# A woven attention and maxout kernel: new order of the steps from batch 4's last sums on, and tiles in listed buffers

## The chip, the cores and the metric

The kernel runs on one core of one Trainium2 chip. The metric is the device time of one execution in microseconds, lower is better. The core has five engines with a queue of instructions each: TensorE (PE; its weight loads are shown apart as PEld), VectorE (DVE), ScalarE (ACT), GpSimd (POOL) and SyncE (SP), which here only issues DMAs. An engine works through its own queue in order; between engines, semaphores say what has to be finished first.

## What is computed

Attention with pooled keys and values over 8 batches, 8 heads, 576 tokens and 64 dimensions, then a maxout layer over all 8 x 576 = 4608 tokens with 512 channels and 768 hidden units. Cut to what matters:

```python
k_p = k.reshape(B, H, S // 8, 8, D).mean(axis=3)      # 72 keys per head
v_p = v.reshape(B, H, S // 8, 8, D).mean(axis=3)
scores = np.matmul(q, k_p.transpose(0, 1, 3, 2)) / np.sqrt(D)
attn = np.exp(scores - scores.max(-1, keepdims=True))
attn = attn / (attn.sum(-1, keepdims=True) + 1e-09)
x = np.matmul(attn, v_p)           # then (batch, token) x (head, dim)
h = np.maximum(np.maximum(x @ w1, x @ w2), x @ w3)
out = h @ w_out
```

## The kernel before

The work has two halves that run through each other. The attention goes by batches 0 to 7 of 576 tokens, the maxout layer by blocks 0 to 8 of 512 tokens, so a block needs tokens of one or two batches: block 5 needs batch 4 from its third chunk on and two chunks of batch 5, block 6 the rest of batch 5 and the first chunk of batch 6. Nothing is scheduled automatically. The order on every engine is the order in which the program emits its instructions, and that order is written out by hand as lists of short names. `MIDDLE` covers blocks 1 to 5 and the batches beside them, `ORDER` (run by `weave`) the outputs of block 5, the hidden part of blocks 6 to 8, the rest of batches 6 and 7 and the outputs of block 7. The emission order binds only instructions of one engine among themselves; a DMA on SP's queue, for instance, waits for the DMAs emitted before it on SP, and for its data.

A name with `-` emits the first part of a step, as a rule its matmuls, and parks its second part, as a rule the eviction of the PSUM result by ACT or DVE; the same name with `+` emits the parked part. Without a sign both follow at once. A number before a colon or stroke is the batch or the block:

- `b:T`, in `do`: one DMA transpose on SP of the whole query tile, `qT<-qb` (line 352). It needs batch b's q loaded. Batches 0 to 2 turn their queries on TensorE.
- `b:k`: three transposes of the pooled keys on TensorE and four copies into `kz` (line 215), all on ACT for batches 4 to 6, for batch 7 two on DVE and then two on ACT.
- `b:s0`, `b:s3`, `b:s6`: scores of three, three and two heads (line 229); their later parts are exponentials on ACT (line 234). Batch 7 instead has nine flat steps `s70` to `s78` of 512 columns, after batch 6's scores.
- `b:v0` to `b:v4`: attention times values for a chunk of 128 tokens (line 305), then reciprocal and product on DVE (lines 313, 315) give `xn`. `b:x0` to `b:x4`: a DMA transpose on SP of that chunk into the token buffer, `xT<-xn` (line 290), for batches above 2. In `ORDER` the colon is left out (`v62`, `x62`).
- `n/h`: one of a block's twelve hidden pieces, four matmuls of 512 columns (line 423); alternately ACT takes the relu of one (line 429) and DVE the maximum with the next (line 431). They use three PSUM buffers, tag `pw`.
- `n/1` to `n/7`: the seven products by which a block's output is formed, ten matmuls each (line 769), copied on ACT (line 780) or added on DVE (line 783). They need the sums `a1` to `a4` of tokens and `b1` to `b4` of hidden units (DVE, line 668). When all parts of a half are there, SP stores it (line 718). In `ORDER` these are `o1` to `o7`.
- In `ORDER`, `1a` to `7c`: seven products of four matmuls (line 846) for each of three groups a, b, c, that make blocks 6, 7 and 8's hidden units; ACT and DVE combine them (lines 823, 826, 855, 859). `T` forms the token differences they need (line 620), on DVE for block 6 and on GpSimd for blocks 7 and 8. `F` is half of an output tile of block 6 (lines 471, 475).
- `q7<`, `k7<`, `v7<`: GpSimd issues a load of that batch from memory, `q` of 576 KB with a cast to bf16, k and v with a cast to f16. It waits for the latest hidden piece or product emitted, and for the landing of the latest `T`. There are two buffers for each of q, k and v.
- `k6+2`, `v5+2`: the next two of the four additions by which GpSimd pools keys or values (lines 163, 163, 165, 167). `!` notes the latest DVE sum of those steps that take a gate; the next of these additions then waits for that sum. `f` is one difference of weights on DVE (lines 592, 601).

The tiles come from pools whose tags have a number of buffers that are used in rotation: PSUM has `att` (two), `pw` (three) and `tr` (one) while `MIDDLE` runs, and `pa`, `sc` (two each), `bc`, `po` and `val` (one each) while `ORDER` runs. A tile waits until the buffer's last tile has been read.

The names that the prediction uses: `5:x3`, `6:x0` and `7:T` on SP's queue, `s70` (`psf`), `2a`, `T`, the folds of `v 7` (`vpool`), block 4's products `4/3` and `4/4` with their stores.

Of the kernel before, what the change touches and what calls it, by code (L numbers as in the profile page):

```python
# [14 lines left out]
def kernel(
# [553 lines left out]
    pools.append(stage.enter_context(tc.tile_pool(name="psp", bufs=1, space=PSUM,  # L569
                                                  reuse_waits="tile")))  # L570
# [3 lines left out]

    def block(n, plan, stages):

        for slot, end in enumerate(part for stage in stages for part in stage(n)):
            if end:
                end()
            for b, steps in plan.get(slot, ()):  # L580
                if b < B:
                    do(b, steps)
# [476 lines left out]
```

## Time and profile before

| | us |
|---|---|
| runs of the kernel before | 226.75, 226.52, 225.45 (median 226.52) |
| profiled execution: span from the first to the last instruction | 224.5 |
| TensorE busy in the span | 213.0 |
| last matmul's end to the span's end (220.7 to 224.5) | 3.8 |
| a load of q, k, v from issue to landing (median of 7) | 7.7, 8.0, 11.9 |

The profiled execution is shown by its span; the runs' times also hold what lies before and after it, 2.0 us for the median. The profile's page has busy time by engine, groups of instructions by line, and DMA queues; the trace behind it also answers who waited for whom, and what ran in a stretch of time. Times in it are counted from the span's start. An instruction on SP is the issue of a DMA: its duration is how long the issue held SP, and the landing comes later. Matmuls overlap in the pipeline, so a row of four matmuls is longer than the distance to the next row. In brackets behind a row stands the idle time of its engine before it, and what ended that, as inferred from semaphores.

How the engines were busy over the span, in tenths, for 40 equal slices:

```profile
PE   7788999999999999999999999999799999999993
DVE  3658989037998795885679468629767977878940
ACT  2267524846784577266735845493694445564330
POOL 7974300999957969787685669794292903881020
DMA  6999999989749799739987998599420645200265
```

Counted from 0, slice 27 (from 151.5 us) begins the stretch in which the change's two lists meet; slices 28 and 29 are 157 to 168 us.

### The profile page before, as it was taken

What the parts mean: (1) busy time and instruction counts of PE and PEld (TensorE: products, weight loads), DVE (VectorE), ACT (ScalarE), POOL (GpSimd) and SP (SyncE); (2) the same over time, 40 slices, a digit from 0 to 9 for tenths busy, and PEclk for the clock granted to TensorE, in tenths of its full rate; (3) what the DMA queues carried; (4) which work ended last, traced back from release to release, by engine and by line L of the source; (5) the groups of instructions that cost most, each with busy time, mean ns of one, the idle gap of its engine ahead of it and who ended that gap; (6) DMA issues with size and microseconds to landing.
All of it is one profiled execution on the core that took longest, in us unless ns stands there. A gap on an engine that the chain in (4) does not pass through costs nothing.

```text
span 224.5 us, 4870 instructions
## 1 busy us (share of the span) xinstructions
PE 213.0 (95%) x1884; PEld 147.3 (66%) x1885; DVE 157.9 (70%) x308; ACT 123.2 (55%) x239; POOL 140.9 (63%) x121
## 2 busy tenths in 40 slices
PE   7788999999999999999999999999799999999993
PEld 2477744458659744964685478447589667788882
DVE  3658989037998795885679468629767977878940
ACT  2267524846784577266735845493694445564330
POOL 7974300999957969787685669794292903881020
PEclk9999999999999999999999999999999999999999
DMA  6999999989749799739987998599420645200265
GB/s 167 212 197 196 207 208 207 204 170 226 135 106 190 131 177 248 124 58 212 252 93 157 227 217 140 75 257 157 103 56 19 167 100 110 47 0 3 65 198 161
DMA packets 47303, 33.55 MB, mean 149 GB/s; under 512 B 26992, under 2 KB 42288, under 8 KB 47280
## 3 DMA queue, kind: packets, MB, share of 16 engines
q0 software_dynamic: 16944, 16.98, 47.2%
q1 hardware_dynamic: 29888, 15.87, 31.2%
q10 hardware_dynamic: 448, 0.39, 0.7%
q8 instruction: 15, 0.25, 0.4%
q14 instruction: 8, 0.07, 0.1%
HBM read 34.60 MB, written 9.44 MB: 196 GB/s over the span
## 4 chain that ended last, share of the span: by engine, by line
PE 69%; DMA 12%; POOL 8%; DVE 6%; ACT 2%; issue 1%; POOLq 0%; DVEq 0%; ACTq 0%
PE pw L423 22%; PE oA L769 13%; DMA vt<-in_v_dram 8%; PE oC L769 7%; PE pA L846 6%; DMA mw<-in_moe_w_dram 4%; PE pav L305 4%; PE oB L769 3%; PE psc L229 3%; PE po L475 3%; PE pC L846 3%; POOL half L163 2%; PE po L471 2%; DVE xn L315 1%; POOL mw L108 1%
## 5 line engine op out<-in xcount | busy, mean ns | idle before, releaser
L423 PE MATMUL pw<-xT,mw 128*128 128x512 f16 (+1 forms) x336 | 68.4, 349 | 0.2 <-ACT xT L299 0.2
L423 PEld LDWEIGHTS <-mw 128*128 128x128 f16 x336 | 30.7, 98 | 26.3 <-issue 1.8
L163 POOL TENSOR_TENSOR half<-vt 72x1024 f32<-72x1024 f16 (+1 forms) x12 | 29.1, 2443 | 20.5 <-DMA vt<-in_v_dram 13.2
L431 DVE TENSOR_TENSOR hT<-t,pw 128x512 f16<-128x512 f16 (+1 forms) x42 | 25.4, 608 | 21.4 <-PE pw L423 12.1
L234 ACT ACTIVATE et<-psc 72x512 f16<-72x512 f32 (+2 forms) x66 | 33.9, 571 | 9.0 <-PE psc L229 8.9
L165 POOL TENSOR_TENSOR half<-half 72x1024 f32<-72x1024 f32 (+1 forms) x13 | 28.1, 2165 | 10.4 <-DVE rcp L313 5.2
L429 ACT ACTIVATE t<-pw 128x512 f16<-128x512 f32 (+1 forms) x42 | 22.6, 538 | 17.0 <-PE pw L423 16.5
L315 DVE TENSOR_TENSOR xn<-pav,rcp 128x512 f16<-128x512 f32 x40 | 27.7, 691 | 1.4
L163 POOL TENSOR_TENSOR half<-ktFalse 96x768 f32<-96x768 f16 (+1 forms) x11 | 19.3, 1767 | 3.9 <-issue 3.8
L855 ACT CAST pad<-pA 128x512 f16<-128x512 f32 x27 | 15.1, 586 | 11.6 <-PE pA L846 9.1
L780 ACT COPY osb<-oA 128x512 f32<-128x512 f32 x20 | 11.8, 588 | 17.4 <-PE oA L769 17.2
L769 PEld LDWEIGHTS <-tt 128*128 128x128 f16 x200 | 18.9, 98 | 2.4
L229 PEld LDWEIGHTS <-kz 64*128 64x128 bf16 (+1 forms) x161 | 8.8, 95 | 12.4 <-issue 8.0
L305 PE MATMUL pav<-vp,et 72*128 72x65 f16 x320 | 16.4, 194 | 0.6 <-DVE xn L315 0.2
L305 PEld LDWEIGHTS <-et 72*128 72x128 f16 x320 | 15.0, 98 | 3.0 <-issue 1.3
L313 DVE RECIPROCAL rcp<-pav 128x8 f32<-128x8 f32 x40 | 8.1, 202 | 10.9 <-PE pav L305 10.8
L846 PEld LDWEIGHTS <-sw 128*128 128x128 f16 x144 | 13.8, 97 | 2.7 <-issue 0.2
L826 DVE SCALAR_TENSOR_TENSOR hT<-pad 128x512 f16<-128x512 f16 x18 | 14.0, 784 | 1.1 <-ACT pad L859 0.5
L823 DVE TENSOR_TENSOR pad<-pad,pC 128x512 f16<-128x512 f16 x18 | 12.3, 682 | 3.5 <-PE pC L846 2.7
L229 PE MATMUL psc<-qT,kz 64*128 64x256 bf16 (+5 forms) x138 | 13.2, 263 | 1.0 <-DVE qT L197 0.9
L620 POOL TENSOR_TENSOR pad<-xT 128x256 f16<-128x256 f16 x8 | 5.5, 689 | 13.0 <-DMA xT<-xn 13.0
L769 PEld LDWEIGHTS <-hT 128*128 128x128 f16 x126 | 12.3, 98 | 1.4
(122 smaller groups left out, 400.6 us busy)
## 6 DMA issues: line engine op xcount, KB each, us to landing
out_dram<-osb SPq DMA_DIRECT2D x32, 128.0 KB, 4.3
ktFalse<-in_k_dram POOLq DMA_DIRECT2D x7, 576.0 KB, 8.0
qb<-in_q_dram POOLq DMA_DIRECT2D x7, 576.0 KB, 7.7
vt<-in_v_dram POOLq DMA_DIRECT2D x7, 576.0 KB, 11.9
out_dram<-osb SPq DMA_DIRECT2D x11, 256.0 KB, 6.7
mw<-in_moe_w_dram POOLq DMA_DIRECT2D x9, 256.0 KB, 9.4
ktTrue<-in_k_dram SPq DMA_DIRECT2D x3, 384.0 KB, 5.4
out_dram<-ob SPq DMA_DIRECT2D x8, 128.0 KB, 2.8
```

What stands on the lines that cost most here:

```text
L163: yield e.tensor_tensor(out=f[:, at], in0=t[:, at, 0:4, :], in1=t[:, at, 4:8, :], op=ALU.add)
L165: yield e.tensor_tensor(out=f[:, :, 0:2, :], in0=f[:, :, 0:2, :], in1=f[:, :, 2:4, :], op=ALU.add)
L229: nc.tensor.matmul(out, kz_all[b % 2][f % 2][rows, h, :], qTs[b][rows, n + i0:n + i1, 64 * (h % 2):64 * (h % 2) + 64], start=True, stop=True)
L234: nc.scalar.activation(out=out, in_=in_, func=FT.Exp, scale=1.0 / 64.0)
L305: nc.tensor.matmul(pav[:, h // 4, 65 * (h % 4):65 * (h % 4) + 65], ets[b][:, h, c0:c0 + 128], vp_all[:, b, h, :], start=True, stop=True)
L315: nc.vector.tensor_tensor(out=xn, in0=pv[:, :, :, 0:D], in1=rcp.to_broadcast([128, 2, 4, D]), op=ALU.mult)
L423: mm = nc.tensor.matmul(pw, w_sb[wi][:, kc, bass.ts(jc, 128)], x[:, kc], start=(kc == 0), stop=(kc == KCH - 1))
L429: yield lambda t=t, pw=pw: nc.scalar.activation(out=t, in_=pw, func=FT.Relu)
L431: yield lambda t=t, pw=pw: nc.vector.tensor_tensor(out=hT[:, jc, c0:c1], in0=t, in1=pw, op=ALU.max)
L769: nc.tensor.matmul(p, left, right, stop=(r == 4), skip_group_check=True, start=(i in FIRST and r == 0 and (m == 0 or n == LAST)))
L846: mm = nc.tensor.matmul(p[:, w], a[:, kc, bass.ts(g, 128)], b[:, kc, :], start=(i in FIRST and w + kc == 0), stop=(w + kc == 2), skip_grou ...
L855: nc.scalar.copy(out=kept(i, g), in_=p)
```

## The change

Every step stays, with its instructions; the order and the buffers are new.

1. The hand-written plan of block 0 (`block`, with batch 1's first steps) becomes names at the head of `MIDDLE`, in the same order, with the loads of batch 3 and the folds of batch 2's k and v behind it (`k3<<` is a load without the waits). The folds of batches 1 and 2 keep their three additions, those above 2 their four.
2. From `5:T` on, `MIDDLE` is in a new order, and all of `ORDER` is. `4/3` and `4/4` are copied out and stored ahead of `5:x3` on SP, where they came behind `5:x4`; `q7<` and `v7<` stand between the additions of batch 6's values, where they came in block 5; `k7<` stands ahead of batch 5's last value additions; `7:T` stands behind `6:x0`, where it stood in batch 6's scores ahead of it. Batch 5's to 7's additions are split into single steps at other places, with other gates.
3. The class `Turns` gives each tile of a tag the buffer that a list (`SLOTS`) names for it, where rotation would have given the next. Tags without a list rotate as before. The number of buffers of each tag is the same.

```diff
+class Turns:
+    def __init__(self, pool, key, turns, bufs=1):
+        self.pool, self.key, self.bufs, self.turns, self.count = pool, key, bufs, turns, {}
+    def tile(self, shape, dtype, name, tag, bufs=None):
+        i = self.count.get(tag, 0)
+        self.count[tag] = i + 1
+        turns = self.turns.get(f"{self.key}.{tag}", "")
+        at = int(turns[i]) if i < len(turns) else i % (bufs or self.bufs)
+        return self.pool.tile(shape, dtype, name=name, tag=f"{tag}.{at}", bufs=1)
...
+    SLOTS = """
+        ps0.att:0120212012012 sb3.xn:0123450123450123450123450123450123540125
+        psp.pw:012012012021021021021201201201201201202102010210120121021021
+        psp.pw:02120120120120120101012010210210202012012012
+        psp.att:010101010101010101010101010101101010101010101010101010101010
+        psp.att:1010101001010101 sb3.osb:01201021021201 psq.sc:010110101010101010110101
+        psq.pa:0101010100101
+    """
...
-    sb3 = ctx.enter_context(tc.tile_pool(name="sb3", bufs=3))
+    sb3 = Turns(ctx.enter_context(tc.tile_pool(name="sb3", bufs=1)), "sb3", seats, 3)
...
-    block(0, {0: [(0, "v2")], 1: [(0, "v3")], 3: [(0, "x2 x3 w1 v4")], 6: [(0, "x4 d1")], 9: [(0, "w2")], 10: [(0, "d2")], 11: [(0, "w3")], 12: [(0, "w4")], 14: [(0, "w5 z")],
...
-    load_k(3, nc.gpsimd)
-    load_v(3, nc.gpsimd)
-    load_q(3)
-    fold_k(2, nc.gpsimd)
-    fold_v(2)
...
-        if name[2:] == "<":
+        if name[2:3] == "<":
...
+            if name[2:] == "<":
+                for x in (mms[-1], *turned):
+                    after([op], x)
...
     ORDER = """
-        b1 o1- 2a- b3 o1+ k7- b2 1a- 1b- v62- 1a+ k7+ 2a+ b4 T o6- s70- o6+ o2- s70+ o2+ 6a-
-        s71- o5- 7a- s72- 7a+ vpool s71+ 6a+ 1b+ s72+ v62+ s73- v63- 5a- v63+ s74- 6b- x62
-        s73+ s75- s74+ 5a+ v64 s76- s75+ x63 s76+ s77- 4a- s77+ s78- 3a- 4a+ 6b+ s78+ 2c-
-        o7- o5+ 2b- o7+ x64 3a+ 1c- 5b- v70- o3- v70+ 1c+ x70 6c- 2b+ 6c+ 5b+ v71- o4- 2c+
-        3b- o3+ o4+ 2a- T 7b- v71+ 7b+ x71 5c- 3b+ 2b- 5c+ v72- 4b- 1a 4b+ 3c- 7c- 2a+ 7c+
-        v72+ 3c+ F 1b- 4c 1b+ v73 x72 6a- 2b+ 6b- 6a+ F 7a- 5a- F 5a+ 6b+ v74- 3a- v74+ x73
-        7a+ 3a+ x74 F 1c- 4a- 1c+ 4a+ 2c- 5b 6c- 7b- 6c+ 7b+ 3b- T F 3b+ 2c+ 5c- 1a- 5c+ 4b
-        1a+ F 7c 2a- 3c- 2c- 2a+ 3c+ 4c- 6a 4c+ 1b- H 2b- 5a- h 1b+ 5a+ 6b- 7a 3a 6b+ o1 1c-
-        5b- 4a- 5b+ o2- 1c+ 6c- 4a+ 6c+ 7b- 2b+ 7b+ 3b- o6- 2c+ 5c- o6+ o2+ 4b- 5c+ o5- 4b+
-        o5+ 7c o7- 3b+ 3c- 4c- o7+ o3- 4c+ o4- 3c+ o3+ o4+
+        2a- 1a- b1 b3 1a+ o1 k7- 1b- 2a+ b2 o2- k7+ o6- v62- T 6a- o6+ s70- o5- vpool 1b+ s71- b4
+        s70+ v62+ v63- 6a+ 5a- x62 s72- 7a- o2+ o5+ v63+ s71+ 6b- s73- 7a+ v64- 5a+ s75- 3a- s74-
+        s72+ 4a- s73+ s75+ 6b+ s77- v64+ o3- s78- s74+ 4a+ x64 o7 s76- 2b- 1c- 2c- s77+ 2b+ 3a+
+        s78+ s76+ v70- 5b- o4- x63 1c+ v70+ 2c+ 5b+ 3b- 6c- v71- x70 o4+ 3b+ 7b v71+ 1a- 6c+ 5c
+        4b- o3+ 2a- 4b+ v72- 3c- v72+ F 7c- 1b- v73- T 2b- 1a+ 2a+ x71 7c+ 2c- v73+ 6a- 3c+ 1b+ 4c
+        v74- 6b- 6a+ 2b+ x72 x73 5a F 3a- 7a- 2b- F 6b+ 7a+ 5b- v74+ 3a+ x74 1c 4a 5b+ F 7b- 6c-
+        7b+ 2c+ 3b- F 4b- 2a- 6c+ 3b+ 1a- 5c- 4b+ 7c- 1a+ 5c+ F 7c+ 2a+ 3c- T 6a- 4c 1b- 3c+ 2c-
+        6a+ 1b+ H 5a 6b- 7a- 6b+ 3a- o1- h 1c- 7a+ 5b- 3a+ 4a- o2- o1+ 1c+ 7b- 2b+ 5b+ o6- 4a+ 7b+
+        6c- 4b- 2c+ o6+ o7- 6c+ 5c- 4b+ 7c- 5c+ o5- 7c+ 3c- o5+ o2+ 3b- o7+ 4c- o3- 3c+ o4- 3b+
+        4c+ o3+ o4+
...
     MIDDLE = """
...
-        5:T 3/7+ 4:v2- 3/5- 4:v2+ 4:x2 4:v3- 3/5+ 4:v3+ 4:v4 5:k 4:x3 3/3 4:x4 3/4 4/h- q6< 4/h+ 4/h- 4/a1 4/a2 f 4/h+ 4/h- 4/a3 4/a4 ! v5+2 4/h- f 4/h+ k7< 4/h+ 5:s0- 5:s0+
-        4/h- 4/h- 5:s0+ 5:s0+ 4/h+ 5:s0+ 4/h+ 6:T 4/h- 5:s3- 4/h+ 5:s3+ 5:s3+ 5:s3+ 4/h- 5:s3+
-        4/h+ 4/h- 4/b1 4/h+ 4/h ! k6+2 5:s6- 5:s6+ 4/h 4/h 4/b3 4/b2 4/b4 5:s6+ ! k6+2 4/1-
-        v6+2 5:v0 4/2- 4/1+ 5:x0 5:v1- 4/6- 5:v1+ 4/2+ 5:x1 5:v2 4/7- 4/6+ 4/5- 5:x2 5:v3 4/7+ 4/5+ 6:k 5:x3 5:v4 4/3- 5:x4 4/4- 4/3+ 4/4+ 5/h q7< 5/a1 v7< 5/h- 5/a2 5/h- 5/a3
-        5/h+ 5/h+ 5/a4 ! v6+2 5/h- 6:s0- 6:s0+ 5/h+ 6:s0+ 5/h- 6:s0+ 6:s0+ 5/h- 5/h- k7+4 5/h+
-        5/h+ 6:s3- 5/h+ 7:T 6:s3+ 5/h- 6:s3+ 5/h- 6:s3+ 6:s3+ 5/h+ 6:s6- 5/h+ 6:s6+ 6:s6+ 5/h
-        5/h- 6:v0 5/h+ 5/h- 6:x0 6:v1- 5/h+ 6:v1+ 6:x1
+        3/2- 4:v0+ 4:x0 4:v1 3/6- 3/2+ 4:x1 3/6+ 3/7- 5:T 3/7+ 4:v2- 3/5- 4:v2+ ! 3/5+ 5:k- 4:v3-
+        4:v4- 4:v3+ 5:k+ 4/h- 4:v4+ q6< 4/a1 4/h+ 3/3- 4/h- 4/h- 3/4- 4/a2 4/h+ 4:x2 4/h- 5:s0-
+        k7< 4/a3 v5+1 f v5+1 3/4+ 4/h+ f 5:s0+ 4/h- 4:x3 4/h+ 4/h- 4/h- 5:s0+ 4:x4 5:s0+ 5:s0+
+        4/h+ 4/h- 4/a4 4/h+ 5:s3- 6:T 4/h- 4/h- ! 3/3+ 4/h- 4/h+ k6+1 5:s3+ 4/h+ 4/h+ 5:s3+ 4/b1
+        5:s3+ k6+1 5:s3+ 4/h+ 4/h+ 4/h 5:s6- 5:s6+ 4/b2 5:s6+ ! 4/1- 4/2- k6+1 4/b3 5:v0- k6+1
+        5:v0+ 5:x0 v6+1 q7< 4/1+ 4/2+ 4/6- v6+1 5:v1- 4/6+ 5:v1+ 5:x1 4/7- 5:v2- 4/7+ 5:v2+ 4/5-
+        v7< 4/b4 5:v3- 6:k- 5:v4- 4/5+ 5:v4+ 4/3- 5:v3+ 5/a3 5/h- 5/a1 6:k+ 5/h- 5:x2 6:s0- 5/h+
+        6:s0+ 6:s0+ 4/4- 6:s0+ 5/h- 6:s0+ 5/h+ 6:s3- 5/h- 4/3+ 5/h- 6:s3+ 4/4+ 5:x3 5/h- 6:s6-
+        5/h- ! 5/h+ 6:s3+ 5/h- 6:s3+ v6+2 k7+1 5/h+ 6:s3+ 5/a2 5/h+ 5/h- 5/h+ 6:s6+ 5/a4 5/h+
+        6:s6+ 5/h- 5/h+ 5/h+ 6:v0- 5/h+ k7+1 6:v1- 5:x4 6:v0+ 6:x0 5/h- k7+1 5/h- k7+1 7:T 6:v1+
+        6:x1 5/h+ 5/h+
...
-                parts(name, lambda: next(pieces[n]))
+                parts(name, lambda: next(pieces[n]) or (lambda: None))
+            elif n == 0 and step == "p":
```

More of the change, by code (lines that the diff above doesn't have):

```diff
@@ L568 @@
     first.close()
[L569 to L570 removed]
+    pools.append(Turns(stage.enter_context(tc.tile_pool(name="psp", bufs=1, space=PSUM,
+                                                  reuse_waits="tile")), "psp", seats))
     turn_w(0, nc.scalar.copy)
[L575 to L582, printed above, removed]
     HALF = NB // 2
```

60 lines of the change are left out of this document (33 added, 27 removed).

## The prediction

> **What bounds the kernel now.** I read the page first, then the windows, TensorE's waits, and the timelines of SyncE, VectorE and GpSimd about the weakest stretch. Columns of the windows: stretch, its length, then busy time and count for TensorE, its weight loads, VectorE, ScalarE and GpSimd, the granted clock, DMA share and GB/s.
>
> ```profile
> span 224.5 us, 4870 instructions
> PE 213.0 (95%) x1884; PEld 147.3 (66%) x1885; DVE 157.9 (70%) x308; ACT 123.2 (55%) x239; POOL 140.9 (63%) x121
> 50.00:116.00 66.00, 65.57 (x604) 44.15 (x603) 50.75 (x101) 39.62 (x80) 53.25 (x35) 1.00 0.86 165
> 116.00:153.50 37.50, 37.45 (x308) 22.50 (x307) 23.57 (x47) 23.33 (x46) 29.80 (x20) 1.00 0.96 175
> 153.50:182.00 28.50, 25.79 (x273) 21.72 (x270) 23.70 (x45) 16.04 (x30) 14.84 (x13) 1.00 0.52 99
> 182.00:210.90 28.90, 28.90 (x249) 23.61 (x247) 23.66 (x38) 15.50 (x28) 12.55 (x16) 1.00 0.17 37
> PE psf L229 <- ACT osb L780: 1.5, 1, 1.5
> PE psf L229 <- ACT et L234: 0.5, 1, 0.5
> PE pC L846 <- DVE pad L823: 0.4, 1, 0.4
> PE pav L305 <- DVE xn L315: 0.2, 1, 0.2
> ```
>
> TensorE is the bound: from 50 to 210.9 us it is idle for 0.43 + 0.05 + 2.71 + 0.00 = 3.19 us. The diff keeps every step and moves it, so no matmul goes away, and the matmuls' clock is 1.00 throughout. A reordering can thus give back at most the idle time where it reorders, which starts just after 116 us (the second transposed batch below): 0.05 + 2.71. The four waits account for 1.5 + 0.5 + 0.4 + 0.2 = 2.6 us of the 2.71, all between 157 and 181 us, at the seam where the middle list ends and the last list begins.
>
> ```profile
> 149.44 7.44 SPq L352 DMA_TRANSPOSE qT<-qb  x1
> 156.98 2.52 SPq L290 DMA_TRANSPOSE xT<-xn  x2
> 153.52 0.60 PE L769 MATMUL oA<-wm,xT 128*128 128x256 f16 x4
> 159.07 0.38 PE L229 MATMUL psf<-qT,kz 128*128 128x320 bf16 x2 [1.49 <-ACT osb L780]
> 159.55 0.43 DVE L620 TENSOR_TENSOR pad<-xT 128x512 f16<-128x512 f16 x1 [1.01 <-DMA xT<-xn]
> 161.24 4.19 POOL L163 TENSOR_TENSOR half<-vt 72x1024 f32<-72x1024 f16 x2 [6.95 <-DVE pad L620]
> ```
>
> One knot explains them. SyncE hands batch 7's query transpose (7:T) to the DMA at 149.44 and is held by it for 7.44 us, so the token transpose 6:x0 behind it starts only at 156.98. Block 6's differences (T, line 620) wait for it until 159.55, and GpSimd's fold of v 7 waits for T until 161.24. The first flat scores (s70, psf) start at 159.07. The trace blames a ScalarE copy, but the query lands at about that time:
>
> ```profile
> DMA to landing us min/median/max: 9.5/9.5/9.5
> DMA to landing us min/median/max: 4.8/4.8/4.8
> L352 SPq DMA_TRANSPOSE qT<-qb x5: 1990/5311/7440, 61.3 to 149.4; - x5
> DMA to landing us min/median/max: 4.0/8.9/10.1
> 137.22 4.20 POOL L163 TENSOR_TENSOR half<-vt 72x1024 f32<-72x1024 f16 x2
> 142.22 0.79 POOL L99 DMA_DIRECT2D qb<-in_q_dram  x1 [0.80 <-PE pw L423]
> 143.44 0.85 POOL L91 DMA_DIRECT2D vt<-in_v_dram  x1 [0.44 <-issue]
> vt<-in_v_dram POOLq DMA_DIRECT2D x7, 576.0 KB, 11.9
> qb<-in_q_dram POOLq DMA_DIRECT2D x7, 576.0 KB, 7.7
> ```
>
> The first landing is 7:T's (149.44 + 9.5 = 158.9), the second that of 5:T (issued at 116.2), the last pair is over all five. 7:T ran beside the load of v 7 (143.44 + 11.9 = 155.3); 5:T ran with the DMA engines partly idle.
>
> **The change, part by part.** The listed buffers, and the earlier blocks being moved into the list, leave the steps before 116 us in their order and the buffers' number as it was; the work there hides them already (0.43 us idle in 66), so I take nothing, with 0 to 0.4 us either way.
>
> *7:T behind 6:x0.* Durations of steps on TensorE:
>
> ```profile
> 141.05 3.45 PE pw L423 x16
> 159.45 1.09 PE oB L769 x10
> 168.84 0.44 PE pB L846 x4
> 170.15 0.26 PE pav L305 x8
> 155.05 0.29 PE L202 MATMUL pkt<-ident,kp 96*128 96x96 bf16 x3
> 152.84 0.69 DVE L315 TENSOR_TENSOR xn<-pav,rcp 128x512 f16<-128x512 f32 x1
> ```
>
> A hidden piece is 3.45/4 = 0.86 us, an output product 1.09, a block product 0.44, a values step 0.26, the key transpose at most 0.29 (0.15 pipelined). The last list starts on TensorE at 153.52 in both orders, if nothing earlier is late. Behind 6:v0 the new order has 6:v1 and two hidden pieces, 0.26 + 2 x 0.86 = 1.98 us, so 6:v0 ends at 151.5; its normalised tile follows about 1.0 later (now: values begun at 152.14, tile done at 153.5), up to 0.6 more if a hidden piece's maximum is ahead on VectorE. So 6:x0 is issued at 152.5 to 153.1 and takes 2.52/2 = 1.26: 7:T starts between 153.8 and 154.4 and T can start near 156 to 157 rather than 159.55. T's late input and GpSimd's late start (the 0.4 and 0.2, and part of the 0.5) go with it. What is late next? s70 itself. Before it the new list has 2a, 1a, 1b, 6a (4 x 0.44), o1, o2, o6 (3 x 1.09), k7 (0.15) and v62 (0.26): 5.4 us, so TensorE wants the query at 158.9. At 4.8 us to landing it is there at 158.6 to 159.2, so 0 to 0.3 us of wait; at 9.5 us it is there at 163.3 to 163.9, so 4.4 to 5.0. I take the 4.8: the three loads are the last ones and all come sooner. In the new list q 7 goes out behind the first of v 6's two opening additions and v 7 behind the second (now 137.22, 4.20 for both): 137.22 + 2.10 = 139.3, and with 0.79 for the issue 139.3 + 0.8 + 2.1 = 142.2. The two transfers now end 155.3 - 142.2 = 13.1 us after the first issue, so then near 152.4, before 7:T starts. That cover is thin: 1.4 to 2 us.
>
> By the Trainium skill, page "DMA: Bandwidth & Descriptors", section "Latency and other measured facts", a DMA transpose moves 261 GB/s at its slower rate; 590 KB of queries would take an estimated 2.3 us whatever else runs, and s70 would never wait. The trace disagrees: no query transpose landed in under 4.0 us, and three of five took 8.9 or more.
>
> *Block 4's stores ahead of 5:x3.* In the new order the stores of block 4 stand on SyncE's queue ahead of 5:x3, 5:x4, 6:x0 and 7:T; before, the list has all five token transposes of batch 5 ahead of them.
>
> ```profile
> 142.67 3.06 SPq L718 DMA_DIRECT2D out_dram<-osb  x4
> xT<-xn SPq DMA_TRANSPOSE x27, 2.4
> 123.03 1.68 SPq L290 DMA_TRANSPOSE xT<-xn  x1
> xT<-xn SPq DMA_TRANSPOSE x1, 6.6
> ```
>
> Behind the copy of 4/3 the list has eight hidden pieces, 6:s6 (about 0.4) and two values steps, 7.8 us, so SyncE's wait for it ends near 145.7; four stores take 3.06, and 5:x3 goes out at 148.8. It is needed by the first step of the last list (2a, at 153.52). At the usual 2.4 us it lands at 151.2. At 6.6, which is the transpose that followed block 3's stores at 123.03 while loads ran, it lands at 155.4 and TensorE waits 1.9. I take 0.6: the case is nearer the slow row by what is ahead, but it is one row of 27. A wait here gives s70 the same time more, so the two don't add.
>
> *GpSimd's folds beside VectorE's sums.* Before, a gate kept most pairs apart; in the new order v 5's second half runs beside a weight difference, k 6's and v 6's beside block 4's b1 and b4 and block 5's a1 and a3, k 7's beside a2 and a4.
>
> ```profile
> 81.89 2.53 POOL L165 TENSOR_TENSOR half<-half 72x1024 f32<-72x1024 f32 x1 [1.88 <-DVE sw L592]
> 83.53 1.31 DVE L592 TENSOR_TENSOR sw<-mw,sw 128x768 f16<-128x768 f16 x1
> 122.81 0.55 DVE L592 TENSOR_TENSOR sw<-mw,sw 128x768 f16<-128x768 f16 x1
> ```
>
> The same difference took 1.31 us behind a running fold, which ended at 84.42, and 0.55 otherwise: 0.76 lost. Seven such meetings at 0 to 0.76 (up to a whole fold, 2.5, at worst) make 0 to 5.3 us on VectorE over 30 us, where it is busy for 23.57 of 37.5. TensorE feels it only where a PSUM buffer is the last one free; three buffers for hidden pieces cover two pieces, 1.7 us. I take 0.2 on TensorE, with 0 to 2 as bounds. The Trainium skill, page "SBUF — State Buffer", section "SBUF: two separate sides", says of VectorE and GpSimd that the shared port pair is a lock held for the whole instruction and that the loser fully blocks. The trace agrees (the 1.31); by the page a sum that arrives first among GpSimd's 2.5 us loses all of it, which is the worst case above.
>
> *The second half of the last list* (products of blocks 6 to 8).
>
> ```profile
> 181.45 1.46 PE L475 MATMUL po<-mwo,hT 128*128 128x512 f16 x6
> 181.50 0.69 DVE L826 SCALAR_TENSOR_TENSOR hT<-pad 128x512 f16<-128x512 f16 x1
> ```
>
> The second half of the first output tile (po, 181.45) reads all six rows of block 6's maxima, and VectorE writes the last at 181.50 to 182.19, just ahead of the last matmuls that read it: no slack today, after 2.6 us in which VectorE could catch up. The new order starts VectorE's chain earlier by T's gain (about 2.6, 159.55 to 157), and TensorE comes earlier by what it no longer waits, at most 2.6; in the new list the tile's half stands two block products and a values step later than before (1.1 us), with as many steps for VectorE moved ahead of it. I take 0.6 us of wait there, 0 to 1.2. After 182 both orders are full (28.90 of 28.90), and the tail is untouched.
>
> **Sum.** 2.6 us of waits go; 0.1 (s70) + 0.6 (5:x3) + 0.2 (folds) + 0.6 (maximum) = 1.5 come back, the last partly under the second, so 1.1 to 1.5. Net -1.1 to -1.5, from a span of 224.5 to 223.0 to 223.4. The runs' median is 226.52, 2.0 above the span, which I take as what lies around it: 225.0 to 225.4, and I forecast 225.0.
>
> **Rivals.** (a) *All waits go and none returns*, if 5:x3 lands in 2.4 us, the median of 27, and the folds miss the sums: 226.52 - 2.6 = 223.9 (-1.15%). For it speaks that each late input of the seam moves ahead at once; against it, that VectorE's chain has no spare time. (b) *VectorE pays for the folds*, the lock above at its upper bound: 2 us on TensorE, with the 0.6 for 5:x3: 226.5, no change. For it: the 1.31 row; against: VectorE is 63% busy there, and two hidden pieces' time covers most meetings. (c) *7:T lands late* and the change is slower. Place: s70, which in TensorE's order holds everything behind it. It decides from a landing over 4.9 us after issue; three of five query transposes took 8.9, 9.5 and 10.1, 7:T's beside the load of v 7. If v 7 or block 4's stores are still under way at 154, 9.5 to 10.1 us from 154.4 put s70 at 163.9 to 164.5, a wait of 5.0 to 5.6; with the 2.6 gone the time is 226.5 + 2.4 to 3.0 = 228.9 to 229.5.
>
> **Chances.** A measurement of this kernel can tell about 1% (2.3 us) from no change. Forecast 0.35 (its own range 224.3 to 225.9), (a) 0.25, (b) 0.15, (c) 0.25. Faster by over 1% is (a) and the edge of the forecast: 0.27. Slower by over 1% is (c), nearly all: 0.25. Within 1%: 0.48. The range takes in (a), (b) and most of (c): 223.5 to 229.0.
>
> **What would show it.** Right: 6:x0 ahead of 7:T on SyncE near 153, T on VectorE near 157, v 7's fold near 159, q 7 and v 7 issued by 139.5 and 142.5, TensorE idle under 1.5 us from 153.5 to 182. Wrong: s70 waiting for the query (c); 2a waiting for a token transpose behind stores; VectorE's sums of 1.3 us and more with TensorE waiting for hidden pieces' buffers before 153 (b). A new wait before 116 us would say that the buffer lists matter, which I priced at nothing.

## The result and the profile after

| | before | after |
|---|---|---|
| median of the runs, us | 225.98 (225.45 to 229.34, 7 runs) | 224.76 (224.06 to 232.1, 7 runs) |
| ratio after to before | | 0.993, interval 0.9902 to 0.9958 |
| profiled execution, span, us | 224.5 | 222.6 |
| its own time, us | | 224.31 |

The change makes the kernel 0.7% faster, less than the 1% that the prediction counts as told from no change, though the interval of the ratio leaves out 1. The median of before, 226.52 where the prediction had three runs, is 225.98 over seven. Some executions took 228 us and longer (one of seven before, one of seven after and none of the eight of e10, three of six of e1, four of ten of e8, three of eight of e11); medians hold these runs, ratios leave them out, and four profiles below (e1, e2, e4 and e5) come from such runs, so that there the waits and the ratio belong to different runs.

In the changed kernel the lines of the code stand further down: line 423 is now 450 (hidden pieces), 290 is 317 (token transposes), 352 is 379 (query transposes), 718 is 736 (stores), 769 is 787 and 846 is 864 (products), 229 is 256 (scores), 620 is 638 and 668 is 686 (differences and sums on VectorE).

First the head of the page, then the windows that the prediction showed of before, with the same columns, then TensorE's one wait of over 0.2 us between 50 and 210 us.

```profile
span 222.6 us, 4865 instructions
PE 212.2 (95%) x1885; PEld 147.2 (66%) x1885; DVE 164.0 (74%) x308; ACT 122.6 (55%) x239; POOL 141.0 (63%) x121
```

```profile
50.00:116.00 66.00, 65.58 (x604) 44.18 (x603) 50.65 (x101) 39.63 (x80) 53.21 (x35) 1.00 0.87 166
116.00:153.50 37.50, 35.99 (x303) 21.93 (x301) 28.12 (x46) 22.58 (x45) 31.31 (x20) 1.00 1.00 179
153.50:182.00 28.50, 28.50 (x296) 23.88 (x295) 26.00 (x50) 17.23 (x33) 13.95 (x12) 1.00 0.48 94
182.00:210.90 28.90, 28.89 (x246) 23.76 (x245) 24.27 (x38) 15.21 (x29) 12.10 (x16) 1.00 0.20 44
```

```profile
PE pw L450 <- issue: 1.5, 1, 1.5
```

The seam, 153.5 to 182 us, was 25.79 of 28.50 busy and is now full: all four waits are gone. But the stretch before it, which was full (37.45 of 37.50), now has 1.51 us of idle time, in one wait for a hidden piece. TensorE's share did not change from 50 to 116 us, nor from 182 to 210.9.

What became of SyncE's knot is read in the timelines of SyncE, GpSimd, VectorE and TensorE, and in the landing of 7:T:

```profile
136.63 4.05 SPq L317 DMA_TRANSPOSE xT<-xn  x3
145.89 3.17 SPq L736 DMA_DIRECT2D out_dram<-osb  x4
149.52 6.10 SPq L317 DMA_TRANSPOSE xT<-xn  x3
155.72 1.83 SPq L379 DMA_TRANSPOSE qT<-qb  x1
139.43 0.80 POOL L126 DMA_DIRECT2D qb<-in_q_dram  x1
142.31 0.87 POOL L118 DMA_DIRECT2D vt<-in_v_dram  x1
158.62 0.41 DVE L638 TENSOR_TENSOR pad<-xT 128x512 f16<-128x512 f16 x1
154.84 0.60 PE L864 MATMUL pB<-xT,mw 128*128 128x256 f16 x4
160.30 0.38 PE L256 MATMUL psf<-qT,kz 128*128 128x320 bf16 x2
```

```profile
DMA to landing us min/median/max: 4.0/4.0/4.0
```

7:T (line 379) starts at 155.72, holds SyncE for 1.83 us where it held it for 7.44, and lands in 4.0 where it took 9.5: at 159.7, 0.6 before s70 needs it at 160.30. The token transpose 6:x0 is the last of the three issued from 149.52 on, and T starts at 158.62. The last list's first step, 2a, stands at 154.84; before, that list began at 153.52. So the list begins 1.32 us later and the kernel ends earlier all the same: the last matmul ended at 220.7 and now ends at 218.69 (217.87 + 0.82 in the timeline). From the list's start to that end it was 67.2 us and is 63.85, 3.3 less.

The new wait, in TensorE's and SyncE's timelines, and then the landing of the second token transpose of batch 4:

```profile
116.64 0.68 PE L332 MATMUL pav<-vp,et 72*128 72x65 f16 x16
118.81 1.02 PE L450 MATMUL pw<-xT,mw 128*128 128x512 f16 x4 [1.49 <-issue]
113.62 2.52 SPq L317 DMA_TRANSPOSE xT<-xn  x2
```

```profile
xT<-xn SPq DMA_TRANSPOSE x1, 3.8
```

Block 4's first hidden piece, 4/h0, reads the tokens that 4:x0 and 4:x1 bring. The two issues start at 113.62, so 4:x1 is issued near 114.9 and lands 3.8 later, at 118.7; the piece starts at 118.81. The trace names no releaser ("issue"), but the times meet, and they meet in all six profiles that have this wait: the second transpose's landing, worked out from its own issue, comes 0.04 to 0.13 us before the piece, with landings of 3.8 to 4.4 us and waits of 1.49 to 2.15 (after, e10, e11, e4, e7, e8). In the old order 3/3 and 3/4 stood ahead of this piece, two products of ten matmuls of 1.09 us each; the new order has them behind it, and with them 2.18 us of cover (other work between a transfer's issue and its reader) are gone.

### The profile page after: what moved, and what is told of

Same layout as the page of the kernel before. It is cut to its first block, busy times and chain, and to the rows that moved or that the text cites. A ratio compares the mean times of both kernels' runs of the same rounds, so it can differ in the third digit from the quotient of the medians.

```text
span 222.6 us, 4865 instructions
## 1 busy us (share of the span) xinstructions
PE 212.2 (95%) x1885; PEld 147.2 (66%) x1885; DVE 164.0 (74%) x308; ACT 122.6 (55%) x239; POOL 141.0 (63%) x121
## 4 chain that ended last, share of the span: by engine, by line
PE 88%; DVE 4%; DMA 3%; issue 1%; ACT 1%; SPq 0%; ACTq 0%
PE pw L450 27%; PE oA L787 14%; PE pA L864 7%; PE oC L787 7%; PE po L502 5%; PE psc L256 4%; PE pav L332 4%; PE pC L864 4%; PE oB L787 3%; PE po L498 3%; DMA ktTrue<-in_k_dram 3%; PE pm L437 2%; PE pB L864 2%; PE pqt L222 2%; PE pxt L323 2%; DVE xn L342 1%
## 5 line engine op out<-in xcount | busy, mean ns | idle before, releaser
L190 POOL TENSOR_TENSOR half<-ktFalse 96x768 f32<-96x768 f16 (+1 forms) x11 | 19.8, 1813 | 4.5 <-issue 4.3
L844 DVE SCALAR_TENSOR_TENSOR hT<-pad 128x512 f16<-128x512 f16 x18 | 14.5, 816 | 0.9 <-ACT pad L877 0.6
```

What stands on the lines that cost most here:

```text
L190: yield e.tensor_tensor(out=f[:, at], in0=t[:, at, 0:4, :], in1=t[:, at, 4:8, :], op=ALU.add)
```

## The experiments

All are edits of the order lists, of the changed kernel unless it is said otherwise. The waits are those of TensorE in one profile each, in us: at 4/h0, at block 5's first hidden piece 5/h0, and from the last list's start on.

| run | ratio to before, interval | 4/h0 | 5/h0 | last list |
|---|---|---|---|---|
| before | 1 | 0 | 0 | 2.6 |
| after | 0.993 (0.9902 to 0.9958) | 1.5 | 0 | 0 |
| e1 3/3, 3/4 first | 0.9895 (0.9849 to 0.994) | 0 | 3.9 | 0.3 |
| e2 their copies too | 1.0326 (1.0262 to 1.039) | 0 | 13.1 | 0 |
| e3 only the last list new | 0.9969 (0.9935 to 1.0003) | 0 | 0 | 1.6 |
| e4 only the middle new | 1.0034 (1.001 to 1.0058) | 1.8 | 2.2 | 2.0 |
| e5 e1, q 7 and v 7 late | 1.0005 (0.9972 to 1.0037) | | | |
| e6 e5, k 7 late too | 1.0149 (1.0104 to 1.0195) | 0 | 0 | 2.9 |
| e7 v 7 alone late | 1.0055 (1.0019 to 1.0092) | 2.2 | 0 | 2.8 |
| e8 7:T ahead of 6:x0 | 0.9927 (0.9884 to 0.997) | 1.9 | 0 | 0 |
| e9 e1, q 7 apart, 5:x3 sooner | 0.9887 (0.9863 to 0.991) | 0 | 0.4 | 0 |
| e10 after once more | 0.992 (0.9882 to 0.9959) | 1.5 | 0 | 0 |
| e11 most buffer lists out | 0.998 (0.9944 to 1.0015) | 1.6 | 0 | 0 |
| e12 e9 without 5:x3 | 0.9918 (0.9886 to 0.9949) | 0 | 0 | 1.2 |

### The wait that came in: e1 and e2

**e1_out_first** puts block 3's last two products back ahead of 4/h0:

```diff
-        4:v4- 4:v3+ 5:k+ 4/h- 4:v4+ q6< 4/a1 4/h+ 3/3- 4/h- 4/h- 3/4- 4/a2 4/h+ 4:x2 4/h- 5:s0-
+        4:v4- 4:v3+ 5:k+ 3/3- 3/4- 4/h- 4:v4+ q6< 4/a1 4/h+ 4/h- 4/h- 4/a2 4/h+ 4:x2 4/h- 5:s0-
```

> Changed kernel, with block 3's last two output products (3/3, 3/4) put ahead of block 4's first hidden piece on TensorE. Theory: the 1.49 us that TensorE waits at 117.3 us is for the landing of the token transpose 4:x1 (issued near 114.9, landing near 118.7); with 2 x 1.09 us of other work ahead of it the piece comes at about 119.6 and the wait goes: span 221.0 to 221.5, ratio to before 0.985 to 0.988, no wait of TensorE over 0.3 us between 116 and 122. Rival: the wait is for a PSUM buffer or for ScalarE's copies of keys; then it stays at 1 us or more and the ratio is 0.992 to 0.994. Third case: three pieces in a row find only two free buffers and 0.5 us comes back: 0.988 to 0.990.

The wait at 4/h0 is gone. That alone doesn't tell the transposes from anything else that is late there by under 2.18 us; together with the landings above, which the piece follows each time, it settles the cause: the piece came too soon for its transposes. The ratio, 0.9895 from three runs, is above the 0.985 to 0.988 expected, and the median, 226.89, is above the changed kernel's: three of the six runs took 229. One of those was profiled, and a larger wait stands further on. The timelines of TensorE, SyncE and GpSimd, then the granted clock over the 40 slices of the page:

```profile
143.73 2.71 PE L450 MATMUL pw<-xT,mw 128*128 128x512 f16 x8 [3.90 <-DMA xT<-xn]
137.79 1.22 SPq L317 DMA_TRANSPOSE xT<-xn  x1
137.90 0.80 POOL L126 DMA_DIRECT2D qb<-in_q_dram  x1
```

```profile
PEclk9999999999999999999999999799999999999999
```

Block 5's first hidden piece waits for 5:x1, which went out at 137.79 and took 5.8 us to land (143.6); q 7's load was issued at 137.90, 0.1 us behind it. In the changed kernel 5:x1 went out at 138.16, q 7's load 1.3 us later at 139.43, and 5:x1 landed in 2.5. That this meeting is also what made the other two runs of 229 isn't shown, since they have no profile. Removing the first wait moves everything, the loads too, and brings q 7 up against 5:x1.

**e2_out_first_evict** is e1 with the copy of 3/4 moved ahead as well, so that block 3's stores go sooner:

```diff
-        4:v4- 4:v3+ 5:k+ 3/3- 3/4- 4/h- 4:v4+ q6< 4/a1 4/h+ 4/h- 4/h- 4/a2 4/h+ 4:x2 4/h- 5:s0-
-        k7< 4/a3 v5+1 f v5+1 3/4+ 4/h+ f ...
+        4:v4- 4:v3+ 5:k+ 3/3- 3/4- 4/h- 4:v4+ q6< 4/a1 4/h+ 4/h- 3/4+ 4/h- 4/a2 4/h+ 4:x2 4/h- 5:s0-
+        k7< 4/a3 v5+1 f v5+1 4/h+ f ...
```

> As the run before, with the eviction of 3/4 moved ahead too, so that its buffer comes free sooner. If the buffers bind there, this is faster than the run before by up to 0.5 us; if not, the same within 0.2 us of span (221.0 to 221.5).

The four runs took 233 to 239, where the time of e1 or up to 0.5 us less was expected. Block 3's stores went at 120.52, 4.0 us sooner than in the changed kernel, and met the loads of q 6 and k 7. SyncE's and TensorE's timelines, then two landings:

```profile
120.52 2.00 SPq L736 DMA_DIRECT2D out_dram<-osb  x3
122.57 4.35 SPq L317 DMA_TRANSPOSE xT<-xn  x3
132.98 6.69 SPq L379 DMA_TRANSPOSE qT<-qb  x1
141.18 5.70 SPq L317 DMA_TRANSPOSE xT<-xn  x3
152.67 3.47 PE L450 MATMUL pw<-xT,mw 128*128 128x512 f16 x8 [13.06 <-DMA xT<-xn]
```

```profile
DMA to landing us min/median/max: 14.2/14.9/15.7
DMA to landing us min/median/max: 8.8/9.4/10.0
```

The last two token transposes of batch 4 took 14.2 and 15.7 us to land (first landing row). q 6's load, issued at 121.33, took 11.6, so 6:T went out only at 132.98 and held SyncE for 6.69; batch 5's transposes went at 141.18, again beside q 7's load, and took 8.8 to 10.0 (second row). 5/h0 waited 13.06 us. How the transfers meet decides, not how early each one is.

### Which part of the change earns the gain: e3, e4, e7, e8

**e3_last_list_only** has `MIDDLE` of the kernel before and `ORDER` of the changed one; **e4_middle_list_only** the reverse. In both the buffer lists that belong to the missing half are out.

> The middle list in the order of before (the query transpose 7:T ahead of 6:x0, loads as before), the last list in the new order. Theory (the knot on SyncE's queue makes the seam's waits): 6:x0 still lands near 159.5, T ends near 161, and TensorE waits about 2 us at the first product that reads T (6a, near 158.5); no wait at 117: 0.5 to 1.0 us gained, span 223.5 to 224.0, ratio 0.995 to 0.998. Rival (the last list's own order makes the gain): no wait over 0.5 us at the seam, span 221.2 to 221.8, ratio 0.986 to 0.988.

> The new middle list, the last list in the order of before. Theory: the 1.5 us at 117 stay; at the seam T is early (near 158), but s70 stands 3.9 us after the list's start where the new list has 5.4, and the query lands near 159.7, so s70 waits about 1 us: span 223.3 to 223.9, ratio 0.995 to 0.998. Rival (the middle list makes the whole gain): no wait at the seam, span 222.4 to 222.8, ratio 0.992 to 0.994.

In e3 the two waits in the new last list are `pA` for T's sums, 1.2 us, and one of 0.4; 7:T stands where it stood, holds SyncE for 8.0 us and makes T late. The ratio's interval reaches 1. In e4 the middle's waits come in (1.8 and 2.2, in a run of 231.51 us) and the old last list asks for s70's query 0.9 us too soon; the other runs are no better than before (ratio 1.0034), which missed the expected gain. One more run of e4 took 554.48 us; it has no profile, and nothing here explains it. In e4's profile the wait at 4/h0 also slows the matmuls behind it (line 445 there is 450 in the changed kernel; the window's third number from the end is the granted clock):

```profile
119.07 1.27 PE L445 MATMUL pw<-xT,mw 128*128 128x512 f16 x4 [1.76 <-issue]
120.00:123.00 3.00, 3.00 (x13) 1.76 (x12) 0.76 (x2) 0.60 (x1) 0.84 (x2) 0.50 0.45 95
```

So neither half earns the gain alone: the middle brings the query and 6:x0 in time, and the last list has enough other products ahead of s70 and T.

**e8_T_ahead** undoes only the exchange of 7:T and 6:x0 on SyncE:

```diff
-        6:s6+ 5/h- 5/h+ 5/h+ 6:v0- 5/h+ k7+1 6:v1- 5:x4 6:v0+ 6:x0 5/h- k7+1 5/h- k7+1 7:T 6:v1+
+        6:s6+ 5/h- 5/h+ 5/h+ 6:v0- 5/h+ k7+1 6:v1- 5:x4 6:v0+ 7:T 6:x0 5/h- k7+1 5/h- k7+1 6:v1+
```

> Changed kernel with 7:T put ahead of 6:x0 again on SyncE's queue, the loads staying early. If the order of the two transposes alone makes the seam's gain, 6:x0 lands 4 us or more later, T and v 7's fold with it, and TensorE waits 1.5 to 3 us at the seam: ratio 0.998 to 1.004. Theory: with the loads done, 7:T holds SyncE for 1.8 to 3 us only, so T is late by 0 to 2 us, s70 has its query sooner, and TensorE waits 0 to 0.7 us: ratio 0.992 to 0.996.

```profile
153.50:182.00 28.50, 28.50 (x296) 23.80 (x295) 26.14 (x50) 17.12 (x32) 14.08 (x13) 1.00 0.49 94
```

```profile
152.82 2.41 SPq L379 DMA_TRANSPOSE qT<-qb  x1
158.76 0.41 DVE L638 TENSOR_TENSOR pad<-xT 128x512 f16<-128x512 f16 x1
```

These are the window of the seam, and 7:T and T in the timelines. The seam stays full, 7:T holds SyncE for 2.41 us and lands in 4.0 even ahead of 6:x0, and T starts at 158.76 against 158.62. With the loads early the exchange, the part of the change that the diff shows best, brings nothing; whether it would with late loads was not run.

**e7_v_late** leaves the exchange and puts v 7's load later, behind the last additions of v 6:

```diff
-        v7< 4/b4 5:v3- 6:k- 5:v4- 4/5+ 5:v4+ 4/3- 5:v3+ 5/a3 5/h- 5/a1 6:k+ 5/h- 5:x2 6:s0- 5/h+
+        4/b4 5:v3- 6:k- 5:v4- 4/5+ 5:v4+ 4/3- 5:v3+ 5/a3 5/h- 5/a1 6:k+ 5/h- 5:x2 6:s0- 5/h+
...
-        5/h- ! 5/h+ 6:s3+ 5/h- 6:s3+ v6+2 k7+1 5/h+ 6:s3+ 5/a2 5/h+ 5/h- 5/h+ 6:s6+ 5/a4 5/h+
+        5/h- ! 5/h+ 6:s3+ 5/h- 6:s3+ v6+2 v7< k7+1 5/h+ 6:s3+ 5/a2 5/h+ 5/h- 5/h+ 6:s6+ 5/a4 5/h+
```

> Changed kernel with the last v load put back alone, behind the fold of v 6 (issue near 147 instead of 142.3), so that it is under way when 7:T starts (155.7). Theory (a query transpose beside a load lands in 9 to 10 us): 7:T lands near 165, s70 waits 4 to 5 us, the time is 227.5 to 229, ratio 1.005 to 1.015. Rival (by the page's rate for transposes, or because a transpose needs only its own turn): landing 4 to 5 us, no wait over 0.5 us at s70, ratio 0.992 to 0.995.

SyncE's issue of 7:T in the timeline, and TensorE's largest wait:

```profile
156.12 4.39 SPq L379 DMA_TRANSPOSE qT<-qb  x1
```

```profile
PE pkt L229 <- POOL kp L194: 2.6, 1, 2.6
```

The load was expected near 147 and went out at 152.36, after GpSimd had been idle for 5.12 us until a hidden piece released it; that is 8.9 us later than in the kernel before, too. Beside it the query transpose held SyncE for over 4 us and took 6.5 to land, not the 9 to 10 expected. The price that TensorE paid came from elsewhere: the fold of k 7 stands behind that load on GpSimd and was 2.6 us late; s70, in a list that came 2.6 later, no longer waited. The time fits and the place does not. With e8 this shows that the transpose is quick when the loads are over, whichever stands first. A kernel of the old order with only the loads moved was not run, so what they would bring alone is open.

### How late the loads may be: e5 and e6

**e5_late_qv** is e1 with `q7<` and `v7<` moved behind 5/h0, **e6_late_kqv** has `k7<` behind v 5's second addition too:

```diff
-        5:v0+ 5:x0 v6+1 q7< 4/1+ 4/2+ 4/6- v6+1 5:v1- 4/6+ 5:v1+ 5:x1 4/7- 5:v2- 4/7+ 5:v2+ 4/5-
-        v7< 4/b4 5:v3- 6:k- 5:v4- 4/5+ 5:v4+ 4/3- 5:v3+ 5/a3 5/h- 5/a1 6:k+ 5/h- 5:x2 6:s0- 5/h+
+        5:v0+ 5:x0 v6+1 4/1+ 4/2+ 4/6- v6+1 5:v1- 4/6+ 5:v1+ 5:x1 4/7- 5:v2- 4/7+ 5:v2+ 4/5-
+        4/b4 5:v3- 6:k- 5:v4- 4/5+ 5:v4+ 4/3- 5:v3+ 5/a3 5/h- q7< 5/a1 v7< 6:k+ 5/h- 5:x2 6:s0- 5/h+
...
-        k7< 4/a3 v5+1 f v5+1 3/4+ 4/h+ f ...
+        4/a3 v5+1 f v5+1 k7< 3/4+ 4/h+ f ...
```

> As e1_out_first, but the last q and v loads go out where they did before, behind block 5's first hidden piece (issue near 141 to 142 instead of 138 and 141). Theory (the last loads, sooner, run beside the token transposes 5:x0 and 5:x1 and make them land late at block 5's first hidden piece): 5:x1 lands by 140.5, the 3.9 us wait of e1_out_first goes to 0.6 or less, no disturbed runs at 229, ratio 0.983 to 0.988, span 220.6 to 221.8. 7:T then runs beside the end of v 7's load (until about 154): s70 waits 0 to 2 us, in which case 0.988 to 0.992. Rival (the query transpose 6:T and the stores ahead on SyncE make them late): the wait stays 2 us or more, ratio as e1_out_first, 0.989 or more.

> As e5_late_qv, with k 7's load behind v 5's fold as before (issue near 126.5 instead of 123.4). If k 7's load, beside the load of q 6, is what holds 6:T and the transposes behind it, 6:T lands sooner and the ratio is 0.982 to 0.986; if it is not, the same as e5_late_qv within 0.3 us of span, or later by up to 1 us because k 7's load moves onto 6:T and 5:x0.

e5's time is that of before, no gain where one was expected. Its profile comes from a run of 274.66 us with a granted clock of 0.76, too slow a TensorE to wait for anything, so where e5 loses stays open. e6 is 1.5% slower than before, worse than either case expected, and its profile shows by what. TensorE's waits, then the timelines of SyncE and TensorE:

```profile
PE pB L864 <- DMA xT<-xn: 2.9, 2, 2.5
PE pw L450 <- DVE osb L801: 1.8, 1, 1.8
```

```profile
148.60 2.98 SPq L736 DMA_DIRECT2D out_dram<-osb  x4
152.05 6.28 SPq L317 DMA_TRANSPOSE xT<-xn  x3
160.22 0.60 PE L864 MATMUL pB<-xT,mw 128*128 128x256 f16 x4 [2.50 <-DMA xT<-xn]
```

5/h0 does not wait, but 2a now does, 2.5 us: 5:x3 goes out at 152.05 behind block 4's stores, with v 7's load under way until 159.0 (q 7's landed at 151.3), and lands at 160.2, 8.1 later. Another 1.8 us is a hidden piece that waits while VectorE's addition of an output is late, and from 128 to 131 us, behind that wait and one of 0.5, the granted clock was 0.50. So in this order the loads have a window: not beside 5:x1, and over before 5:x3 and 7:T.

### A version that is faster than both: e9, e10 and e12

**e9_q_apart** is e1 with q 7's load just ahead of v 7's, past the landing of 5:x1, and with 5:x3 and 5:x4 ahead of block 4's stores:

```diff
-        5:v0+ 5:x0 v6+1 q7< 4/1+ 4/2+ 4/6- v6+1 5:v1- 4/6+ 5:v1+ 5:x1 4/7- 5:v2- 4/7+ 5:v2+ 4/5-
-        v7< 4/b4 5:v3- 6:k- 5:v4- 4/5+ 5:v4+ 4/3- 5:v3+ 5/a3 5/h- 5/a1 6:k+ 5/h- 5:x2 6:s0- 5/h+
-        6:s0+ 6:s0+ 4/4- 6:s0+ 5/h- 6:s0+ 5/h+ 6:s3- 5/h- 4/3+ 5/h- 6:s3+ 4/4+ 5:x3 5/h- 6:s6-
+        5:v0+ 5:x0 v6+1 4/1+ 4/2+ 4/6- v6+1 5:v1- 4/6+ 5:v1+ 5:x1 4/7- 5:v2- 4/7+ 5:v2+ 4/5-
+        q7< v7< 4/b4 5:v3- 6:k- 5:v4- 4/5+ 5:v4+ 4/3- 5:v3+ 5/a3 5/h- 5/a1 6:k+ 5/h- 5:x2 5:x3 5:x4 6:s0- 5/h+
+        6:s0+ 6:s0+ 4/4- 6:s0+ 5/h- 6:s0+ 5/h+ 6:s3- 5/h- 4/3+ 5/h- 6:s3+ 4/4+ 5/h- 6:s6-
...
-        6:s6+ 5/h- 5/h+ 5/h+ 6:v0- 5/h+ k7+1 6:v1- 5:x4 6:v0+ 6:x0 ...
+        6:s6+ 5/h- 5/h+ 5/h+ 6:v0- 5/h+ k7+1 6:v1- 6:v0+ 6:x0 ...
```

> As e1_out_first (block 3's last products ahead of block 4's first hidden piece), with the last q load put behind both opening additions of v 6, just ahead of the last v load (issue near 140 instead of 138), and with 5:x3 and 5:x4 ahead of block 4's stores on SyncE. Theory: 5:x1, issued near 137.4, has landed in 2.5 to 3.6 us before the load begins, so block 5's first hidden piece waits 0 to 0.6 us instead of 3.9; the first step of the last list waits for no token transpose; the loads end near 153, before 7:T: span 220.6 to 221.6, time 222.2 to 223.2, ratio 0.980 to 0.986, and no runs at 229 and over. Rival (6:T and the loads ahead of it already make 5:x1 late): a wait of 2 us or more at the same piece, ratio 0.988 or more.

**e10_after_again** is the changed kernel on the same chip.

> The changed kernel itself, beside the others on this chip: ratio 0.990 to 0.995, and by the theory one run in seven or so disturbed to 229 or more, where the last q load starts before 5:x1 has landed.

Two windows of e9, then TensorE's, SyncE's and GpSimd's timelines:

```profile
116.00:153.50 37.50, 37.01 (x305) 22.10 (x304) 27.55 (x48) 22.90 (x46) 31.36 (x20) 1.00 0.97 175
153.50:182.00 28.50, 28.50 (x301) 24.27 (x300) 25.21 (x48) 17.89 (x35) 13.95 (x12) 1.00 0.50 103
```

```profile
140.21 1.89 PE L450 MATMUL pw<-xT,mw 128*128 128x512 f16 x8 [0.44 <-DMA xT<-xn]
137.63 1.22 SPq L317 DMA_TRANSPOSE xT<-xn  x1
140.24 0.80 POOL L126 DMA_DIRECT2D qb<-in_q_dram  x1
```

With q 7 out of its way 5:x1, out at 137.63, lands in 2.4 us, and one wait of 0.44 is left of all that lay between 116 and 182. The six runs took 223.12 to 224.05 (median 223.7), the changed kernel 223.99 to 225.8 (median 224.65, eight runs), so 0.95 us less; the waits by themselves say 1.49 - 0.44 = 1.05. The stores (from 133.7) and 6:T (from 128.2) went out much as in e1, so it was q 7's load, not these, that made 5:x1 late there. 5:x3, out at 140.90, runs beside both loads and takes 10.3 us, but 2a stands at 153.85, 2.6 after its landing. The expected ratio, 0.980 to 0.986, was too good. e10 itself came as expected (0.992), but none of its eight runs took 229 us, where one in seven or so was expected.

**e12_q_apart_alone** is e9 with 5:x3 and 5:x4 left behind block 4's stores, as in the changed kernel.

> This is e9_q_apart without its second edit: 5:x3 and 5:x4 stay behind block 4's stores; the loads of q 7 and v 7 still stand together behind 5:x1, and 3/3 and 3/4 still go ahead of block 4's first hidden piece. Theory: the gain of e9 comes from taking the load of q 7 away from 5:x1, and the place of 5:x3 does not matter, because in the changed kernel it is issued at 149.5, over 5 us ahead of the last list's first step. Then TensorE's waits from 116 to 182 us are again under 0.6 us, the span is 221 to 222.5 and the ratio 0.985 to 0.991. Rival: with the loads later than in the changed kernel, 5:x3 behind the stores now meets the load of v 7 and lands late; then the last list's first step waits for it by 1 to 2.5 us and the ratio is 0.993 to 1.000.

SyncE's and TensorE's timelines:

```profile
145.16 2.91 SPq L736 DMA_DIRECT2D out_dram<-osb  x4
148.53 6.36 SPq L317 DMA_TRANSPOSE xT<-xn  x3
155.45 0.60 PE L864 MATMUL pB<-xT,mw 128*128 128x256 f16 x4 [1.17 <-DMA xT<-xn]
```

The rival was right about the place: 5:x3, out at 148.53, took 6.9 us to land, and 2a waited 1.17 for it. v 7's load, issued straight behind q 7's at 141.8, took 11.7 here (7.3 in the changed kernel, which issued it 2.9 us behind q 7's), so it ran until 153.5. The median, 224.77 (223.69 to 225.21), is that of the changed kernel, and the ratio, 0.9918, lies between the ranges of theory and rival. So the 1 us that e9 gains needs 5:x3 ahead of the stores as well; 5:x3 moved with q 7 left beside 5:x1 was not run.

### The buffer lists: e11

**e11_rotation** takes the lists of `att` in block 0, `xn`, `att`, `osb` and `pa` out of `SLOTS`; those of `pw` and `sc`, which the order needs, stay.

> Changed kernel with five of its seven buffer lists taken out (first stage's att, xn, att of the middle list, osb, pa), so that these tiles rotate; the lists of pw and sc stay, which the order needs. Theory (the lists that can go cost and bring next to nothing): the same as the changed kernel, 0.990 to 0.995. Rival (the lists carry the gain): TensorE waits for buffers of att or pa, 1 us or more, ratio 0.996 to 1.002.

The profiled run (224.66 us, span 223.0) has the waits of the changed kernel, 1.6 at 4/h0 and a full seam. Its ratio, 0.998, is 0.6% above that of e10 on the same chip, with intervals that overlap: it lies outside the range of the theory (0.990 to 0.995) and in the rival's (0.996 to 1.002), whose wait of 1 us or more for a buffer the trace doesn't have. No wait in the trace goes back to the lists, but the runs leave room for a gain of theirs of up to about 1%: open.

## Why the prediction was right, and where it was not

The forecast, 225.0, is 0.24 us from the median, and the span that it gave, 223.0 to 223.4, is 0.4 to 0.8 above the measured 222.6. The sum held, but not by its terms: that the total came out is luck in part. Part of it is the 2.0 us put on top of the span, from the median of three runs and the span of another execution; in the runs with both on record the difference is 1.7 (224.31 and 222.6), which would have made the forecast 224.7 to 225.1.

**The 2.6 us at the seam.** Right, all four went. The loads' times, worked out from the position of v 6's additions (139.3 and 142.2), came at 139.43 and 142.31, and the choice of the quick landing for 7:T (4.8; measured 4.0) was right for the reason given, the loads being over. It also gave credit to the exchange of 7:T and 6:x0, which e8 shows to be worth nothing once that is so.

**The four returns, 1.5 us together.** None came. s70's wait: 0, in the range of 0 to 0.3. 5:x3 behind the stores: 0, in 0 to 1.9, with little to spare, since it went out at 149.52, landed 4.5 us later at 154.0, and 2a started at 154.84. The term is real: e12 pays 1.17 and e6 2.50 for it. Folds: VectorE's busy time between 116 and 153.5 rose from 23.57 to 28.12, 4.55 us and near the upper bound of 5.3, and TensorE did not feel it. The rival (b) had the cost on VectorE about right and its effect on TensorE wrong. Block 6's last maximum: 0, as the full window after 153.5 shows.

**The step that failed** is the clause "The last list starts on TensorE at 153.52 in both orders, if nothing earlier is late". Something earlier was late: 4/h0 by 1.49 us, a wait that the prediction does not have. It counted every step that SyncE's queue was moved past at the seam, but of 3/3 and 3/4 it followed only the sister products of block 4. Those two hid the landing of 4:x1 for 2.18 us; the prediction's own rows of 2.4 and 6.6 us for a token transpose, counted from its issue near 114.9, would have bounded the landing at 117.3 to 121.5, against 117.3 (116.64 + 0.68) where TensorE is free for the piece: a wait of 0 to 4.2. The last list began 1.32 late, T at 158.62 rather than near 157 and v 7's fold at 160.28 rather than near 159.

**The sum by measured terms.** 2.71 us of idle time went and 1.49 came, which makes 1.22; the span fell by 1.9. In the part from the last list's start the path is shorter by 3.3 us, 0.7 more than the 2.6 of waits in it. That fits what a row of four matmuls shows: it lasts 0.60 us while the next starts after 0.44 (154.84, then 155.28 in the timeline), so a gap in TensorE's rows is about 0.16 shorter than what it delays, four times here. The runs bear out the direction and not the whole size: the new last list, from its first row to the last matmul's end, takes 63.85 to 64.28 us in six profiles without a wait in it (after, e8 to e12), and 67.13 in e7 with one wait of 2.63, so one wait costs at least 0.2 more than it shows. By the same measure the wait of 1.49 would delay by 1.65, and the list began only 1.32 late; these 0.3 us are not accounted for, and the spread of 0.4 between profiles is as large. The prediction took 2.6 for the waits, which looks too low; a return sized at 1.5 us for other reasons made up for it.

**The bound at 116 us** held: 65.58 of the 66 us from 50 to 116 are busy, so no wait says that the lists matter there.

**The rival (c)**, a late 7:T, did not occur; the cover that the prediction called thin, 1.4 to 2 us, was there. v 7's load was over by 149.6, and 7:T started at 155.7, later than the 153.8 to 154.4 forecast because the list came late.

## What to carry to other kernels

Before the steps of a hand-written order are exchanged, go through every transfer that is waited for and list how much work stands between its issue and its first reader in the old order and in the new; a step that is moved for other reasons may have been that cover. A load that goes out sooner is worth it where it is over before a transpose on the way to the critical engine starts, and costs where it starts beside one: place loads between the transposes, and expect that removing one wait moves the loads behind it into new company. When a forecast's total comes out right, still check each term against the trace.
